# Fourteen weight pieces decoded in part two instead of part one, without the detour through DRAM

## The chip, the cores and the metric

The kernel runs on one core of a Trainium2 chip. The metric is device time in microseconds (us); lower is better. The kernel before takes 1982.79 us (median of 3 runs, 1981.26 to 1983.64). TensorE (PE) multiplies, VectorE (DVE) and ScalarE (ACT) do elementwise work, GpSimd (POOL) does next to nothing here, and SyncE's queue (SP) issues every DMA.

## What is computed

Three layers follow each other: a Fourier mix along the sequence (4 batches of 3072 tokens, 256 channels), an MoE-like layer with 2048 hidden units, and a channel mix with 1024 hidden units. Cut to what matters here:

```
X = rfft(x, axis=1);  Yr = Xr@w_r - Xi@w_i + b_r;  Yi = Xr@w_i + Xi@w_r + b_i
y = irfft(softshrink(Yr, 0.01) + 1j*softshrink(Yi, 0.01))     # 4 x 3072 x 256
h = y @ w_in;  g = h * tanh(softplus(h));  z = g @ w_out      # w_in 256x2048, w_out 2048x256
zk, zr = mixes of z with the token before it
out = sigmoid(zr @ w_g) * (relu(zk @ w_k)**2 @ w_v)            # w_k 256x1024, w_v 1024x256, w_g 256x256
```

The function h*tanh(softplus(h)) is one ScalarE function, Mish. The weights of the last two layers (w_in, w_out, w_k, w_v, w_g) come as 64-bit floats, which no engine multiplies. They are turned on the chip into two 32-bit tiles each, a rounded high part and the low rest, and every product is taken as three matmuls (high by high, high by low, low by high).

## The kernel before

**Part one** does the Fourier mix in 48 units (`u`), 12 for each batch: matmuls `xps`, `yps` and `bps` on PE, with ScalarE and VectorE between them. Its results go to DRAM (`b_dr`). A background queue of VectorE work (`bg`: `f1_ops` ahead of the transform, `f3_ops` behind it) fills VectorE between the units; `f3_ops` turns `b_dr` into `y_dr` in jobs of half a batch each, in a tile of the pool `g`.

**Part two** does the two other layers in 24 blocks (`j`) of 512 tokens. A block has 16 steps, and step `s` is block `s // 16`. At step `s` the program writes, engine by engine, what belongs to it:

- PE: `emit_H(s)`, six matmuls into a PSUM tile `hps`; then what the table `PLAN` puts at this step (`emit_K`: six matmuls into `kps`; `emit_V`: twelve into `v`; `emit_R`); then `emit_acc(s - 3)`, six matmuls into `a` from `gh`, `gl` and the tile of `w_out` for that step. `hps`, `kps` and `zps` share a ring of four PSUM tiles.
- ScalarE: `act_mish(s - 1)` reads `hps` and writes `u`, and behind it stand the operations that an earlier step left with `later`: `evac` of the block before (`x2s`), `token_mix` (`t`), `split_y` of the next block (`yh`), and the three of a `K` group (`ka`, `kh`, `ka`).
- VectorE: `dve_g(s - 1)` writes `gh` (a cast of `u`) and `gl` (`u` minus `gh`). One operation of the list `vx` is put behind `gh`, one behind `gl`, and the rest after that; where `vx` is empty, `bg` gives one.

In the first block only `H` and `acc` run; its first `K` group stands at step 22, and needs the mixed tokens `xk` from steps 19 and 20.

**Decoding.** Weights are decoded in pieces of 128x512 numbers; `w_in` and `w_out` have eight each, `w_k` and `w_v` four each, `w_g` one. `raw_piece` loads 512 KB into `raw`; `decode` gives six stages. On VectorE: `v0` (an integer operation and a shift-and-or that build `q`), `v1` (`q` limited, times the sign `sg`), `v2` (the low part; two halves for `w_out`). On ScalarE: `a0` (a copy of the high words into `sg`, then Sign), `a1` (Abs of `q`), `a2` (the high part; two halves for `w_out`). The class `Weights` runs pieces as a pipeline: each call of `vec` starts a piece's `v0`, does `v1` of the piece before, and `v2` of the third before; `sca` does `a2` of the second before, `a0` and `a1` of the new one, and loads the next raw piece.

In the kernel before, all 25 pieces are decoded in part one. Five (`w_k` and one of `w_v`) come at units 6 to 14, the other twenty at units 36 to 47, two per unit. The SBUF that `w_k`, `w_v` and `w_g` will use is still taken there, so these nine pieces are written to DRAM (`park_piece`, `w_dr`), and `fetch` reads them back at the start of part two, with 5 DMAs of 512 KB and 16 of 128 KB. In part two there is no decoding.

The helpers on lines 146 (`tt`), 149 (`stt`), 152 (`act`) and 155 (`mm`) issue most instructions, so the profile shows their lines for nearly everything, and groups are told apart by the names of their tiles. In the changed kernel the same helpers stand two lines further down.

Of the kernel before, what the change touches and what calls it, by code (L numbers as in the profile page):

```python
# [10 lines left out]
F32 = mybir.dt.float32  # L11
# [25 lines left out]
START = (20500, 20500)  # L37
SLACK = (2000, 3200)

NPARK = 5  # L40
PARK_AT = (6, 15)

F3_PART1 = {(1, 4): [(0, 0)], (1, 8): [(0, 1)]}
F3_PART2 = {1: (1, 0), 3: (1, 1), 5: (2, 0), 8: (2, 1), 10: (3, 0), 14: (3, 1)}


SPLIT_AT = (13, 14)
# [66 lines left out]
def tile_fft_mix_moe_channel_mix(  # L114
# [41 lines left out]

    dram = pool(ctx, "dram", 1, space=bass.MemoryType.DRAM)
    b_dr = [dram.tile([2, 128, NT, 256], F32, name=f"b_dr{b}") for b in range(NB)]
    w_dr = [dram.tile([128, 2, 512], F32, name=f"w_dr{i}") for i in range(9)]
    y_dr = [dram.tile([2, 128, 24, 128], F32, name=f"y_dr{b}") for b in range(NB)]  # L160

    cst = pool(ctx, "cst", 1)
# [272 lines left out]

    raws = []

    def raw_piece(src):
        p, tag = raws[1][raws[0] % len(raws[1])]
        raws[0] += 1  # L440
        raw = p.tile([128, 512, 2], I32, tag=tag, name="raw", bufs=2)
        nc.sync.dma_start(out=raw.rearrange("p (k f) t -> p k (f t)", k=2),
                          in_=src.bitcast(I32).rearrange("(k p) f -> p k f", p=128))
        return raw

    def decode(raw, parts, scale=1.0):
        hw, lw = raw[:, :, 1], raw[:, :, 0]
        tl = {}

        def a0():  # L450
            sg = tl["sg"] = pools["st"].tile([128, 512], F32, tag="sg", name="sg")
            return [lambda: act(sg.bitcast(I32), hw.bitcast(F32), ACTF.Copy, scale=14000.0),
                    lambda: act(sg, sg.bitcast(I32), ACTF.Sign)]

        def v0():
            q = tl["q"] = pools["st"].tile([128, 512], F32, tag="q", name="q", bufs=3)
            qi = q.bitcast(I32)
            return [lambda: V.tensor_scalar(out=qi, in0=hw, scalar1=0x08000000, scalar2=3,
                                            op0=ALU.bitwise_xor, op1=ALU.logical_shift_left),
                    lambda: stt(qi, lw, 29, qi, ALU.logical_shift_right, ALU.bitwise_or)]  # L460

        def a1():
            return [lambda: act(tl["q"], tl["q"], ACTF.Abs)]

        def v1():
            return [lambda: stt(tl["q"], tl["q"], 3.4e38, tl["sg"], ALU.min, MULT)]

        def a2():
            tl["p"] = parts(tl["q"])
            return [lambda hi=hi, v=v: act(hi, v, ACTF.Copy, scale=scale) for hi, lo, v in tl["p"]]  # L470

        def v2():
            if scale == 1.0:
                return [lambda hi=hi, lo=lo, v=v: tt(lo, v, hi.bitcast(F32), SUB) for hi, lo, v in tl["p"]]
            return [lambda hi=hi, lo=lo, v=v: stt(lo, v, scale, hi.bitcast(F32), MULT, SUB)
                    for hi, lo, v in tl["p"]]

        return a0, v0, v1, a2, v2, a1

    def win_piece(i):  # L480
        raw = raw_piece(w_in[:, 256 * i:256 * i + 256])
        cs = slice(256 * i, 256 * i + 256)
        w = wt["in"]
        return decode(raw, lambda q: [(w[:, 0, :, cs], w[:, 1, :, cs],
                                q.rearrange("p (k f) -> p k f", k=2))])

    def wout_piece(i):
        raw = raw_piece(w_out[256 * i:256 * i + 256, :])

        def parts(q):  # L490
# [3 lines left out]
        return decode(raw, parts)  # L494


    parked = ([w_k[:, 256 * i:256 * i + 256] for i in range(4)]
              + [w_v[256 * i:256 * i + 256, :] for i in range(4)] + [w_g])

    def park_piece(i):  # L500
        raw = raw_piece(parked[i])
        tl = {}

        def parts(q):
            t = tl["t"] = yhl_p.tile([128, 2, 512], F32R, tag="yl", name="wp")
            return [(t[:, 0, :], t[:, 1, :], q)]
        a0, v0, v1, a2, v2, a1 = decode(raw, parts)
        return a0, v0, v1, a2, lambda: v2() + [lambda: nc.sync.dma_start(out=w_dr[i], in_=tl["t"].bitcast(F32))], a1

    def fetch():  # L510
        for i in range(4):
            nc.sync.dma_start(out=wt["v"][:, :, 2 * i:2 * i + 2, :].bitcast(F32),
                              in_=w_dr[4 + i].rearrange("p s (c f) -> p s c f", c=2))
        nc.sync.dma_start(out=wt["g"].bitcast(F32), in_=w_dr[8].rearrange("p s (c f) -> p s c f", c=2))
        for c in range(8):
            wt["k", c] = mat.tile([128, 2, 2, 128], F32R, tag="m", name="wkt")
            src = w_dr[c // 2].rearrange("p s (h k f) -> p s h k f", h=2, k=2)
            for z in range(2):
                nc.sync.dma_start(out=wt["k", c][:, z].bitcast(F32), in_=src[:, z, :, c % 2, :])

    class Weights:

# [48 lines left out]
    def part1():  # L571
        with ExitStack() as es:
# [163 lines left out]
            for u in range(NU):  # L736
                b, t = divmod(u, NT)
                if t == NT - 1 and b + 2 < NB:
                    new_a(b + 2)
                if t == F1_AT[b] and b + 1 < NB:  # L740
                    hs = [f1_ops(As[b + 1], h) for h in range(2)]
                    for i, due in ((slice(14), 0), (slice(14, 24), 4), (slice(24, None), 8)):
                        bg.add(both(*[(h[0] + h[1])[i] for h in hs]), NT * (b + 1) + due)
                bg.jobs += F3_PART1.get((b, t), [])
                bg.step()
                if u == NU - NT - 1:
                    wt["in"] = big.tile([128, 2, 2, 2048], F32R, tag="big", name="win")
                    todo = [lambda: win_piece(0)]
                    for i in range(8):
                        if i < 7:  # L750
                            todo.append(lambda i=i: win_piece(i + 1))
                        todo.append(lambda i=i: wout_piece(i))
                    late = [lambda i=i: park_piece(i) for i in range(NPARK, 9)]
                    wq = Weights(todo[:6] + late + todo[6:])
                    wq.load(3)
                dec = 0
                if b == NB - 1:
                    dec = 2
                elif PARK_AT[0] <= u < PARK_AT[1]:
                    dec = 1  # L760
                    if u == PARK_AT[0]:
                        wq = Weights([lambda i=i: park_piece(i) for i in range(NPARK)])
                        wq.load(2)
                bg.flush(u + 1)
                if u == 6:
                    S.activation(out=mu1, in_=mu, func=ACTF.Copy, scale=-1.0, bias=1.0)
                pe += 1710 * (u + 1 < NU)
                if u + 1 < NU:
                    emit_F(u + 1)
                if u:  # L770
                    post_M(u - 1)
                if dec:
                    emit(wq.vec())
                    bg.clock += 2100
                if u:
# [11 lines left out]
                if dec == 2:  # L787
                    emit(wq.vec())
                    emit(wq.sca(2))
                    bg.clock += 2100  # L790
                emit_M(u)
                pe = max(pe, x_at + 300) + 2770
                y_new = pe + 700
                if u:
                    emit_I(u - 1)
                    pe = max(pe, y_at + 300) + 1710
                x_at, y_at = x_next, y_new
                if b == NB - 1 and t == 10:
                    bg.drain()
                    load_y(0)  # L800
            while wq.busy():
                emit(wq.vec())
                emit(wq.sca(2))
            for h in range(2):
                emit(split_y(0, h)[1])
            post_M(NU - 1)
            post_M2(NU - 1)
            post_I(NU - 2)
            emit_I(NU - 1)
            post_I(NU - 1)  # L810
# [2 lines left out]
    def part2():  # L813
        with ExitStack() as es:
# [18 lines left out]
            xr = (xr_p.tile([128, 2, 512], F32R, name="xrh"), xr_p.tile([128, 2, 512], F32R, name="xrl"))  # L833
            xs = x2_p.tile([128, 1088], F32, name="x2s")[:, 0:1026].rearrange("p (h f) -> p h f", h=2)

            fetch()
            NC = 16
            h_t, u_t, gh, acc, kt = {}, {}, {}, {}, {}
            vps, rt, mix_t = {}, {}, {}
# [137 lines left out]
            for s in range(max(max(plan), max(fin_at)) + 2):  # L977
                j, c = divmod(s, NC)
                if s < NS:
                    if c == 10 and j + 1 < NBLK:  # L980
                        load_y(j + 1)
                    if j in F3_PART2 and c == 0:
                        bg.jobs.append(F3_PART2[j])
                    bg.step()
                    emit_H(s)
                ax, vx = defer.pop(s, ([], []))
# [12 lines left out]
                    act_mish(s - 1)  # L999
                for e in ax:  # L1000
                    e()
                vx = list(vx)
                bg.have = min(bg.have + FILL[0], FILL[1])

# [62 lines left out]
```

## Time and profile before

| what | value |
|---|---|
| median of 3 runs | 1982.79 us |
| profiled execution, its own time | 1981.86 us |
| its span in the trace | 1979.9 us |
| PE busy | 1958.0 us, 99% of the span |
| DVE busy | 1141.4 us, 58% |
| ACT busy | 929.0 us, 47% |
| first matmul of part two | 327.22 us |

All times inside an execution count from the span's start. The time outside the span is 1.96 us. The granted TensorE clock is 1.00 in every slice of the page, so it plays no part. Where a row ends in brackets, they hold the idle time of that engine just before the row, and what ended it. A start-to-start distance of two rows is often a little shorter than the first row's duration, since an engine overlaps the end of one instruction with the start of the next.

### The profile page before, as it was taken

The numbers are of one execution on the slowest core, as the hardware profiler recorded it, in microseconds if no ns is written. First come the engines' busy times: TensorE is split into PE (matmuls) and PEld (weight loads), VectorE is DVE, ScalarE is ACT, GpSimd is POOL, SyncE is SP. The second block draws the span as 40 slices with busy tenths as digits, with TensorE's granted clock in tenths as the row PEclk, the third lists the DMA queues.
The fourth block names the chain that finished last, engine by engine and source line by source line (L and its number), as shares of the span: only waits on it lengthen the run. The fifth ranks groups of instructions, "written<-read, shape, count | busy, mean of one in ns | idle before, by whom it ended". The sixth has DMA issues, their size and how long they took to land.

```text
span 1979.9 us, 25685 instructions
## 1 busy us (share of the span) xinstructions
PE 1958.0 (99%) x10084; PEld 1686.2 (85%) x10084; DVE 1141.4 (58%) x2183; ACT 929.0 (47%) x1525; POOL 13.2 (1%) x28
## 2 busy tenths in 40 slices
PE   6999999999999999999999999999999999999999
PEld 5888888888888888888888888888888888888888
DVE  8999976665654754465375445555544544444444
ACT  2422286344544554454445444444544544454455
POOL 0000000000000000000000000000000000000000
PEclk9999999999999999999999999999999999999999
DMA  9445276111011010101101001011000000000000
GB/s 279 150 138 170 70 245 200 39 32 65 22 33 54 22 44 11 54 22 33 54 22 54 1 22 54 5 33 38 22 1 22 22 11 12 22 23 1 22 11 22
DMA packets 104554, 106.66 MB, mean 54 GB/s; under 512 B 7017, under 2 KB 85489, under 8 KB 103409
## 3 DMA queue, kind: packets, MB, share of 16 engines
q1 hardware_dynamic: 104432, 105.02, 16.7%
q8 instruction: 79, 1.29, 0.3%
q14 instruction: 43, 0.34, 0.1%
HBM read 62.53 MB, written 42.47 MB: 53 GB/s over the span
## 4 chain that ended last, share of the span: by engine, by line
PE 97%; DMA 1%; DVE 1%; ACT 0%; issue 0%; SPq 0%; DVEq 0%; ACTq 0%
PE a L155 26%; PE hps L155 26%; PE v L155 14%; PE kps L155 13%; PE yps L155 7%; PE bps L155 4%; PE xps L155 4%; PE zps L155 3%; DMA a<-in_x_dram 1%; DMA w_dr<-wp 0%; DVE g L146 0%; ACT sg L152 0%; SPq L266 0%; DVE q L149 0%; ACT q L152 0%
## 5 line engine op out<-in xcount | busy, mean ns | idle before, releaser
L863 DVE CAST gh<-u 128x512 fp32r<-128x512 f32 x384 | 163.2, 425 | 747.5 <-PE a L155 598.2
L155 PE MATMUL a<-gh,wo 128*128 128x512 f32 x1536 | 536.3, 390 | 0.0
L155 PE MATMUL hps<-yh,win 128*128 128x512 f32 x1536 | 534.7, 389 | 0.0
L152 ACT ACTIVATE u<-hps 128x512 f32<-128x512 f32 x384 | 229.7, 598 | 525.0 <-PE hps L155 368.8
L155 PEld LDWEIGHTS hps<-yh,win 128*128 128x128 f32 x1536 | 288.3, 188 | 60.3
L155 PEld LDWEIGHTS a<-gh,wo 128*128 128x128 f32 x1536 | 288.4, 188 | 58.0
L155 PE MATMUL a<-gl,wo 128*128 128x512 f32 x768 | 299.9, 390 | 0.0
L155 PE MATMUL hps<-yl,win 128*128 128x512 f32 x768 | 298.8, 389 | 0.0
L155 PE MATMUL kps<-b,wkt 128*128 128x512 f32 x960 | 280.1, 390 | 0.0
L155 PE MATMUL v<-b,kh 128*128 128x256 f32 x1536 | 275.8, 281 | 0.0
L146 DVE TENSOR_TENSOR gl<-u,gh 128x512 fp32r<-128x512 f32 x384 | 263.6, 687 | 3.6
L155 PEld LDWEIGHTS v<-b,kh 128*128 128x128 f32 x1536 | 243.7, 190 | 7.6
L155 PE MATMUL v<-b,kl 128*128 128x256 f32 x768 | 215.8, 281 | 0.0
L155 PEld LDWEIGHTS kps<-b,wkt 128*128 128x128 f32 x960 | 179.1, 188 | 36.1
L152 ACT ACTIVATE ka<-kps 128x512 f32<-128x512 f32 x192 | 115.0, 599 | 185.5 <-PE kps L155 185.5
L155 PEld LDWEIGHTS hps<-yl,win 128*128 128x128 f32 x768 | 144.1, 188 | 29.9
L155 PEld LDWEIGHTS a<-gl,wo 128*128 128x128 f32 x768 | 144.5, 188 | 26.6
L146 DVE TENSOR_TENSOR kl<-ka,kh 128x512 fp32r<-128x512 f32 x192 | 132.5, 690 | 32.8 <-ACT ka L152 19.1
L155 PEld LDWEIGHTS v<-b,kl 128*128 128x128 f32 x768 | 144.1, 188 | 0.0
L152 ACT ACTIVATE ka<-ka 128x512 f32<-128x512 f32 x192 | 121.4, 632 | 6.3
L152 ACT ACTIVATE kh<-ka 128x512 fp32r<-128x512 f32 x192 | 121.4, 632 | 6.3
L146 DVE TENSOR_TENSOR g<-g 128x128 f32<-128x128 f32 (+3 forms) x272 | 107.5, 433 | 1.2
(80 smaller groups left out, 1926.8 us busy)
## 6 DMA issues: line engine op xcount, KB each, us to landing
b_dr<-bs SPq DMA_DIRECT2D x48, 256.0 KB, 2.2
g<-b_dr SPq DMA_DIRECT2D x8, 1536.0 KB, 6.8
y<-y_dr SPq DMA_DIRECT2D x48, 256.0 KB, 3.2
out_dram<-r SPq DMA_DIRECT2D x48, 256.0 KB, 2.2
y_dr<-g SPq DMA_DIRECT2D x80, 64.0 KB, 1.6
w_dr<-wp SPq DMA_DIRECT2D x9, 512.0 KB, 5.9
a<-in_x_dram SPq DMA_DIRECT2D x8, 512.0 KB, 6.2
y_dr<-g SPq DMA_DIRECT2D x32, 128.0 KB, 1.9
```

What stands on the lines that cost most here:

```text
L146: V.tensor_tensor(out=o, in0=a, in1=b, op=op)
L152: S.activation(out=o, in_=i, func=f, **kw)
L155: T.matmul(out=o, lhsT=l, rhs=r, start=start, stop=stop, **kw)
L863: return [lambda: V.tensor_copy(hi, u), lambda: tt(lo, u, hi.bitcast(F32), SUB)]
```

## The change

- Eleven pieces (eight of `w_in`, three of `w_out`) stay in part one, one per unit from unit 34 on. The other fourteen (five of `w_out`, then four of `w_k`, four of `w_v`, one of `w_g`) are decoded in part two, one every second step from step 0 to step 26, and their pipeline ends at step 32.
- `park_piece`, `fetch` and the tiles `w_dr` go. The decoded parts are written where the matmuls read them.
- The decode's working tiles in part two are slices of one tile of the pool `g` (named `stage`): one slot for `sg`, three for `q`, two for `raw`. In part one `sg` keeps its two buffers.
- The `f3_ops` jobs of part two start at given steps instead of given blocks. The first moves from step 16 to step 34, the second from step 48 to 50; the others keep theirs.
- At the end of part one the last `yb` is written before the first block's `split_y`.

```diff
-NPARK = 5
-PARK_AT = (6, 15)
+NWO = 3
+DEC_STEPS = range(0, 34, 2)
-F3_PART2 = {1: (1, 0), 3: (1, 1), 5: (2, 0), 8: (2, 1), 10: (3, 0), 14: (3, 1)}
+F3_PART2 = {34: (1, 0), 50: (1, 1), 80: (2, 0), 128: (2, 1), 160: (3, 0), 224: (3, 1)}
...
+    def stage(tag, bufs):
+        if "slots" in pools:
+            slots, at = pools["slots"]
+            at[tag] += 1
+            return slots[tag][at[tag] % len(slots[tag])]
+        return pools["st"].tile([128, 512], F32, tag=tag, name=tag, bufs=bufs)
...
         def a0():
-            sg = tl["sg"] = pools["st"].tile([128, 512], F32, tag="sg", name="sg")
+            sg = tl["sg"] = stage("sg", 2)
             return [lambda: act(sg.bitcast(I32), hw.bitcast(F32), ACTF.Copy, scale=14000.0),
                     lambda: act(sg, sg.bitcast(I32), ACTF.Sign)]
...
-                    late = [lambda i=i: park_piece(i) for i in range(NPARK, 9)]
-                    wq = Weights(todo[:6] + late + todo[6:])
+                if u == NU - NT - 3:
+                    wq = Weights([lambda i=i: win_piece(i) for i in range(8)] +
+                                 [lambda i=i: wout_piece(i) for i in range(NWO)])
                     wq.load(3)
...
+            post_M(NU - 1)
+            post_M2(NU - 1)
             for h in range(2):
                 emit(split_y(0, h)[1])
-            post_M(NU - 1)
-            post_M2(NU - 1)
...
-            fetch()
+            for c in range(8):
+                wt["k", c] = mat.tile([128, 2, 2, 128], F32R, tag="m", name="wkt")
+            G = g_p.tile([128, 8, 512], F32, tag="g", name="stage")
+            slots = {"sg": [G[:, 0, :]], "q": [G[:, i, :] for i in (1, 2, 3)],
+                     "raw": [G[:, 4:6, :], G[:, 6:8, :]]}
+            pools["slots"] = (slots, dict.fromkeys(slots, 0))
+            wq = Weights([lambda i=i: wout_piece(i) for i in range(NWO, 8)] +
+                         [lambda i=i: wk_piece(i) for i in range(4)] +
+                         [lambda i=i: wv_piece(i) for i in range(4)] + [wg_piece])
+            wq.load(2)
...
+                if s in DEC_STEPS and wq.busy():
+                    vx = wq.vec() + list(vx)
+                    later(s + 1, wq.sca(2), [])
```

What this does to the order, at two places. First ScalarE where part two begins. `bs` are the last results of part one, `hps` what PE gives to Mish, `u` what Mish writes; before, these rows stand there:

```order
L152 ACTIVATE yb_2720<-yps_2695 128x512
L152 ACTIVATE bs_2723<-bps_2709 128x512
L152 ACTIVATE bs_2731<-bps_2726 128x512
L152 ACT_TABLE_LOAD
L152 ACTIVATE u_2825<-hps_2811 128x512
L152 ACTIVATE u_2838<-hps_2818 128x512
L152 ACTIVATE u_2851<-hps_2831 128x512
L152 ACTIVATE u_2872<-hps_2844 128x512
```

Now there is a decode between every second pair of Mish operations; this is the fourth piece (steps 7 to 9), where `stage` without `hps` is a stage of the decode, and `wo` a piece of `w_out`:

```order
L154 ACTIVATE u_2701<-hps_2669 128x512
L154 ACTIVATE u_2727<-hps_2694 128x512
L154 ACTIVATE wo_2703<-stage_2575 128x256
L154 ACTIVATE wo_2704<-stage_2575 128x256
L154 ACTIVATE stage_2575<-stage_2575 128x512
L154 ACT_TABLE_LOAD
L154 ACTIVATE stage_2575<-stage_2575 128x512 x2
L154 ACT_TABLE_LOAD
L154 ACTIVATE u_2752<-hps_2720 128x512
```

Sign and Abs (the `x2`) stand between two table loads: Mish and Sign are in different tables. The whole program has 77 table loads instead of 49.

The second place is VectorE at the same steps. Before, only `gh` and `gl` stand there:

```order
L863 CAST gh_2912<-u_2910 128x512
L146 TENSOR_TENSOR gl_2913<-u_2910,gh_2912 128x512
L863 CAST gh_2931<-u_2929 128x512
L146 TENSOR_TENSOR gl_2932<-u_2929,gh_2931 128x512
L863 CAST gh_2950<-u_2948 128x512
```

Now `v2` (`wo`), `v1` (the first row that only names `stage`) and `v0` (the two behind it) stand among them:

```order
L863 CAST gh_2756<-u_2752 128x512
L148 TENSOR_TENSOR wo_2703<-stage_2575,wo_2703 128x256
L148 TENSOR_TENSOR gl_2757<-u_2752,gh_2756 128x512
L148 TENSOR_TENSOR wo_2704<-stage_2575,wo_2704 128x256
L151 SCALAR_TENSOR_TENSOR stage_2575<-stage_2575 128x512
L469 TENSOR_SCALAR stage_2575<-stage_2575 128x512
L151 SCALAR_TENSOR_TENSOR stage_2575<-stage_2575 128x512
L863 CAST gh_2786<-u_2778 128x512
L148 TENSOR_TENSOR gl_2787<-u_2778,gh_2786 128x512
```

So `v1` of a piece now stands on VectorE behind the `gh` and `gl` that read a `u` which ScalarE writes after that piece's Abs. And since `sg` has one slot, the ScalarE copy that starts the next piece is made to wait in the built program for exactly this `v1`.

## Rows read from the trace of the kernel before

**Rows 1.** The page, section 1: engine, busy us (share of span), instructions.

```profile
PE 1958.0 (99%) x10084; PEld 1686.2 (85%) x10084; DVE 1141.4 (58%) x2183; ACT 929.0 (47%) x1525; POOL 13.2 (1%) x28
```

**Rows 2.** Timeline, PE: start us, us, engine, line, instruction, [idle before <-releaser].

```profile
293.47 1.99 PE L155 MATMUL bps<-im,yb 128*128 128x256 f32 x8 [0.26 <-DVE yb L149]
...
332.86 0.39 PE L155 MATMUL a<-gh,wo 128*128 128x512 f32 x1
...
384.54 1.52 PE L155 MATMUL kps<-b,wkt 128*128 128x512 f32 x6
...
395.42 1.52 PE L155 MATMUL kps<-b,wkt 128*128 128x512 f32 x6
```

**Rows 3.** Timelines of SP (two issues) and VectorE (first use); landing of `raw`.

```profile
246.01 1.01 SPq L442 DMA_DIRECT2D raw<-in_moe_w_in_dram  x2
...
328.73 2.57 SPq L512 DMA_DIRECT2D b<-w_dr  x4
...
250.13 0.43 DVE L458 TENSOR_SCALAR q<-raw 128x512 int32<-128x512 int32 x1 [3.60 <-DMA raw<-in_moe_w_in_dram]
...
DMA to landing us min/median/max: 3.8/5.4/7.1
```

**Rows 4.** Timeline, ScalarE: one piece's decode in part one.

```profile
310.59 0.71 ACT L152 ACTIVATE wo<-q 128x256 fp32r<-128x256 f32 x2
311.20 0.66 ACT L152 ACTIVATE sg<-raw 128x512 int32<-128x512 f32 x1
311.89 0.63 ACT L152 ACTIVATE sg<-sg 128x512 f32<-128x512 int32 x1
312.43 0.62 ACT L152 ACTIVATE q<-q 128x512 f32<-128x512 f32 x1
```

**Rows 5.** Timeline, ScalarE: the table load where part two begins.

```profile
327.65 0.60 ACT L152 ACTIVATE bs<-bps 128x512 f32<-128x512 f32 x1 [1.18 <-PE bps L155]
328.27 1.28 ACT L152 ACT_TABLE_LOAD   x1
329.56 0.60 ACT L152 ACTIVATE u<-hps 128x512 f32<-128x512 f32 x1
```

**Rows 6.** Timeline, VectorE: the decode's operations, `gh`, `gl`, and a half-width operation.

```profile
309.42 0.69 DVE L149 SCALAR_TENSOR_TENSOR q<-q,sg 128x512 f32<-128x512 f32 x1 [0.26 <-ACT q L152]
310.03 0.42 DVE L458 TENSOR_SCALAR q<-raw 128x512 int32<-128x512 int32 x1
310.48 0.69 DVE L149 SCALAR_TENSOR_TENSOR q<-raw,q 128x512 int32<-128x512 int32 x1
...
330.20 0.43 DVE L863 CAST gh<-u 128x512 fp32r<-128x512 f32 x1 [4.72 <-ACT u L152]
...
420.43 0.43 DVE L863 CAST gh<-u 128x512 fp32r<-128x512 f32 x1 [2.27 <-PE a L155]
420.78 0.42 DVE L146 TENSOR_TENSOR g<-g 128x256 f32<-128x256 f32 x1
421.11 0.69 DVE L146 TENSOR_TENSOR gl<-u,gh 128x512 fp32r<-128x512 f32 x1
```

**Rows 7.** Timeline, VectorE and then ScalarE: a token mix, and a `u` that waited.

```profile
380.84 0.74 DVE L149 SCALAR_TENSOR_TENSOR t<-x2s,mu,t 128x512 f32<-128x512 f32 x1
381.50 0.68 DVE L146 TENSOR_TENSOR gl<-u,gh 128x512 fp32r<-128x512 f32 x1
382.10 0.42 DVE L895 CAST b<-t 128x512 fp32r<-128x512 f32 x1
382.56 0.69 DVE L146 TENSOR_TENSOR b<-t,b 128x512 fp32r<-128x512 f32 x1
...
382.30 0.60 ACT L152 ACTIVATE u<-hps 128x512 f32<-128x512 f32 x1 [2.35 <-DVE gl L146]
```

**Rows 8.** Timeline, ScalarE: the first and last operation of a `K` group.

```profile
386.54 0.59 ACT L152 ACTIVATE ka<-kps 128x512 f32<-128x512 f32 x1
...
387.82 0.64 ACT L152 ACTIVATE ka<-ka 128x512 f32<-128x512 f32 x1
```

More of the change, by code (lines that the diff above doesn't have):

```diff
@@ L158, in tile_fft_mix_moe_channel_mix @@
     b_dr = [dram.tile([2, 128, NT, 256], F32, name=f"b_dr{b}") for b in range(NB)]
-    w_dr = [dram.tile([128, 2, 512], F32, name=f"w_dr{i}") for i in range(9)]
     y_dr = [dram.tile([2, 128, 24, 128], F32, name=f"y_dr{b}") for b in range(NB)]
@@ L436, in tile_fft_mix_moe_channel_mix @@
     raws = []
-    def raw_piece(src):
-        p, tag = raws[1][raws[0] % len(raws[1])]
-        raws[0] += 1
-        raw = p.tile([128, 512, 2], I32, tag=tag, name="raw", bufs=2)
+    def stage(tag, bufs):
[4 more added lines that the diff above has]
+        return pools["st"].tile([128, 512], F32, tag=tag, name=tag, bufs=bufs)
+    def raw_piece(src):
+        if "slots" in pools:
+            raw = stage("raw", 2).bitcast(I32).rearrange("p a f -> p (a f)").rearrange("p (f t) -> p f t", t=2)
+        else:
+            p, tag = raws[1][raws[0] % len(raws[1])]
+            raws[0] += 1
+            raw = p.tile([128, 512, 2], I32, tag=tag, name="raw", bufs=2)
         nc.sync.dma_start(out=raw.rearrange("p (k f) t -> p k (f t)", k=2),
@@ L455, in v0 @@
         def v0():
-            q = tl["q"] = pools["st"].tile([128, 512], F32, tag="q", name="q", bufs=3)
+            q = tl["q"] = stage("q", 3)
             qi = q.bitcast(I32)
@@ L482, in win_piece @@
         cs = slice(256 * i, 256 * i + 256)
-        w = wt["in"]
-        return decode(raw, lambda q: [(w[:, 0, :, cs], w[:, 1, :, cs],
+        return decode(raw, lambda q: [(wt["in"][:, 0, :, cs], wt["in"][:, 1, :, cs],
                                 q.rearrange("p (k f) -> p k f", k=2))])
@@ L494, in wout_piece, with wk_piece, wv_piece, wg_piece @@
         return decode(raw, parts)
[L497 to L502, printed above, removed]
-        def parts(q):
[L505 to L519, printed above, removed]
+    def wk_piece(i):
+        raw = raw_piece(w_k[:, 256 * i:256 * i + 256])
+        def parts(q):
+            z = q.rearrange("p (k f) -> p k f", k=2)
+            return [(wt["k", 2 * i + c][:, 0, :, :], wt["k", 2 * i + c][:, 1, :, :],
+                     z[:, :, 128 * c:128 * c + 128]) for c in range(2)]
+        return decode(raw, parts)
+    def wv_piece(i):
+        raw = raw_piece(w_v[256 * i:256 * i + 256, :])
+        w = wt["v"][:, :, 2 * i:2 * i + 2, :]
+        return decode(raw, lambda q: [(w[:, 0], w[:, 1], q.rearrange("p (c f) -> p c f", c=2))])
+    def wg_piece():
+        raw = raw_piece(w_g)
+        w = wt["g"]
+        return decode(raw, lambda q: [(w[:, 0], w[:, 1], q.rearrange("p (c f) -> p c f", c=2))])
     class Weights:
@@ L747, in part1 @@
                     wt["in"] = big.tile([128, 2, 2, 2048], F32R, tag="big", name="win")
[L748 to L752, printed above, removed]
-                    late = [lambda i=i: park_piece(i) for i in range(NPARK, 9)]
-                    wq = Weights(todo[:6] + late + todo[6:])
-                    wq.load(3)
[L756 to L763, printed above, removed]
+                if u == NU - NT - 3:
+                    wq = Weights([lambda i=i: win_piece(i) for i in range(8)] +
+                                 [lambda i=i: wout_piece(i) for i in range(NWO)])
+                    wq.load(3)
+                dec = u > NU - NT - 3
                 bg.flush(u + 1)
@@ L786, in part1 @@
                     post_I(u - 2)
[L787 to L790, printed above, removed]
                 emit_M(u)
@@ L981, in part2 @@
                         load_y(j + 1)
-                    if j in F3_PART2 and c == 0:
-                        bg.jobs.append(F3_PART2[j])
+                    if s in F3_PART2:
+                        bg.jobs.append(F3_PART2[s])
                     bg.step()
```

## The prediction

> **What bounds the kernel now.** I read the page first: PE is busy for 1958.0 of 1979.9 us, VectorE for 58% and ScalarE for 47% [rows 1]. Then I went through PE's timeline where pieces are decoded today, units 36 to 47 of part one. PE sat idle there once, for 0.26 us, waiting for VectorE [rows 2]. So today's decode hides behind PE, and so does the detour through DRAM: no row of PE waits for it. Any time that PE loses in part two is added to the end, because behind the first two blocks PE is full again and catches up nothing. The question is therefore only whether the other engines can do the decode inside the first 28 steps as fast as PE goes through them.
>
> PE's pace comes from two rows. Between the first `K` group and the third stand eight groups of six matmuls, and they take 395.42 - 384.54 = 10.88 us [rows 2]: 1.36 a group. A step without K or V is two groups, 2.72 us, so a pair of steps, in which one piece is decoded, lasts 5.44 us.
>
> **What is removed.** The idle 0.26 us may go: -0.3. The fourteen pieces' work in part one, nine DMAs to DRAM and 21 back were hidden; they give nothing. The new order at the end of part one is `yb` first and `split_y` after, and those four operations last about as long as the last `bps` group; I take 0, at most 0.5. The later `f3_ops` job falls into steps where VectorE's average load is 58% [rows 1]; 0 to 1.
>
> **The start of part two.** `v0` of the first piece is the first thing on VectorE, ahead of `gh` of step 0, and it waits for its raw data. SP is in order, and these loads stand behind the last `b_dr` store, where the first `fetch` DMA was issued at 328.73. In part one a raw issue at 246.01 was first used at 250.13, 4.1 us later [rows 3]. So the data are there at T = 332.9; with the longest landing, 7.1 us [rows 3], at 335.8. Before, the first `acc` began at 332.86 [rows 2], so some stall is certain at once.
>
> **The cost of one piece on ScalarE.** From the copy into `sg`: 0.69 to Sign's place [rows 4], a table load of 1.29 start to start [rows 5], 0.54 from Sign to Abs, 0.62 for Abs with 0.02 before the next load (as behind `bs`) [rows 4, 5], again 1.29, then Mish. That makes D = 0.69 + 1.29 + 0.54 + 0.64 + 1.29 = 4.45 us. With two Mish operations about 0.5 apart (Sign to Abs is 0.54) and the two halves of `w_out` (0.61) [rows 4] ScalarE has 1.0 + 0.61 + 4.45 = 6.06 us of work a pair, more than PE's 5.44 already.
>
> The Trainium skill speaks against this change here: "ScalarE: Activation LUTs", section "Table sets: the hidden batching unit", says to group activations by table set and to do all of one set before switching. The 1.28 us of the load agree with its section "What ACT_TABLE_LOAD costs" (1283 ns); it adds a drain of some 1380 ns to every switch, but here the load starts 0.02 us after the end of `bs`, and Mish 0.01 us after the load [rows 5]. By its figure D would be some 2.7 us longer, an estimate; I go by the rows.
>
> **The loop that makes it worse.** `sg` has one slot. The copy of a new piece must wait for `v1` of the piece before, and `v1` stands on VectorE behind `gh` and `gl` of a `u` that ScalarE writes only after that piece's second table load. So decode and Mish cannot overlap. From the start of that `u`: 0.64 to `gh` (329.56 to 330.20) [rows 5, 6]; 0.35 to the first `v2` half, 0.33 to `gl` (as with the half-width operation at 420.78) [rows 6]; 0.60 to the second half (as behind `gl` at 381.50) [rows 7]; 0.33 to `v1`; 0.69 for `v1`; 0.12 until ScalarE goes on (`gl` ends at 382.18, `u` starts at 382.30) [rows 7]. Sum 3.06, and then D: **7.51 us a pair, against PE's 5.44**. For the second and third piece there is no `v2` yet, and `gh` to `v1` is 0.35: 0.64 + 0.35 + 0.69 + 0.12 + 4.45 = 6.25.
>
> **The sum along this chain**, counted from T, with `u` numbered by its step:
> - u1 at 4.45; u3 and u5 after two short loops: 16.95.
> - Six loops to u17: 45.06, and a `split_y` copy inside one of them (0.5): 62.5.
> - To u19 a token mix stands ahead of the table load (0.6): 70.6.
> - The mix runs on VectorE late. Its `t` starts on ScalarE at loop time 6.2 and ends at 6.8; then t, `gl`, cast, subtract at 0.66, 0.60, 0.46 and 0.6 [rows 7] end at 9.2, and only then comes the next `gh`: 1.08 behind u19 instead of 0.64. From there 0.35 + 0.33 + 0.60 + 0.33 to `v1`, 0.61 to its neighbour, 0.45 + 0.61 for `v0` [rows 6], then the second half of the mix, 0.66 + 0.46 + 0.69: at 6.2 behind u19 `xk` is complete.
> - The first `K` group can start at T + 70.6 + 6.2 = T + 76.8 = 409.7, where it stood at 384.54: **25.2 us late**.
> - u21 comes 0.44 late: +7.95, 78.6. Before u23 the three operations of a `K` group stand ahead of the table load (386.54 to 388.46, 1.92) [rows 8]: +9.3, 87.9. The third `K` group writes the PSUM tile that u23 frees: T + 87.9 + 0.65 = 421.4 against 395.42: 26.0 late. The group in step 29 waits in the same way for u27, by my count 0.3 us more.
>
> After step 29 no table loads are left but those of Sigmoid, and PE is full again. So the profiled execution of 1981.86 becomes 1981.86 - 0.3 + 26.3 = 2007.9; its time lies 0.93 below the median, which is within the spread of the runs. I predict **2008 us** (+1.3%). Own range: T can be 2.9 later and 0.3 earlier; the nine loops each 0.3 off either way, 2.7; the small terms of the second paragraph +1.5. That is 2004 to 2014.
>
> **Rivals.**
> - *ScalarE's sum alone decides*: if `v1` is never waited for (VectorE ahead of ScalarE, or the wait satisfied early), the loop is 6.06. Then u17 comes at 53.3, u19 (with the `evac` pair, no longer in a gap) at 61.0, `K` at T + 67.2 = 400.1, 15.6 late: 1997 us. The wait is in the built program, and `v1` cannot pass `gh` on its engine; against it. 7%.
> - *The switch is hidden, not slower than before*: if a table load ran while ScalarE waits for VectorE and PE, D would shrink to 0.69 + 0.54 + 0.54 = 1.8 and the loop to about 4.8 us. The point that decides is 5.44: below it PE sets the pace. Only the start is left: `gh` at T + 1.06 and `gl` 0.46 + 0.69 later stand where PE wanted them, at 332.86 and one matmul (0.23) later: some 2 us. Time 1981.86 - 0.3 + 2 = 1983.6, which is no difference that can be measured. Against it: the load in [rows 5] fills ScalarE's time between two operations fully. 3%.
> - *A switch costs twice as much*: a drain as long as the load, 1.28 more a switch, 2.56 a piece. Ten pieces stand before u19, so `K` is 25.6 later than above, and the next two pieces carry 5 more to u23, of which PE's own work hides nothing: 2008 + 31 = 2039. This is what the drain in the Trainium skill, "ScalarE: Activation LUTs", section "What ACT_TABLE_LOAD costs", would do. [Rows 5] show none. 3%.
> - *The change doesn't do what it says*: excluded, as the order shows the loads, and 77 table loads.
>
> **How the numbers follow.** The forecast has 86%, the rivals 7, 3 and 3%, and 1% is for a time that is shorter than before for a reason I don't see. Of the forecast's 86% I put 80 between 2001 and 2014, a little below its own lower end, since small overlaps on ScalarE (0.1 us in each of 30 switches) can add up; to reach further, to 1997 or to 2039, would take in more than 8 times in 10. About 0.2% (4 us) is what a measurement of this kernel can tell from no change: faster by more than that 1%, within it 3%, slower 96%.
>
> **What would show each step.** First use of the raw data near 333. ScalarE nearly full between 335 and 425, with two table loads every 7.5 us, and a wait for VectorE ahead of the copy into `sg`. First `kps` near 410, third near 421. PE's idle time between 330 and 430 about 26 us in sum, first on `gh` and `gl`, later on `xk` and on Mish's PSUM tile; none behind step 30, and part two beginning at 327 as before. The prediction is wrong if the copy into `sg` starts at once after Mish (6.1 us loops), if Mish or Sign start more than 0.1 us behind a load, or if PE stalls after step 30.

## The result, and the profile after

The changed kernel takes **2007.31 us** (median of 4 runs, 2006.83 to 2007.61) where the kernel before takes 1982.30 us in the same comparison (4 runs, 1981.26 to 1983.64). The ratio is 1.0126, with a 95% interval of 1.011 to 1.0142: it is slower by 25 us. The prediction was 2008 us, with a range of 2001 to 2014.

| what | before | after |
|---|---|---|
| profiled execution, its own time | 1981.86 us | 2007.39 us |
| span | 1979.9 us | 2005.4 us |
| PE busy | 1958.0 us, 99% | 1968.3 us, 98% |
| ScalarE busy | 929.0 us, 47% | 965.4 us, 48% |
| first matmul of part two | 327.22 us | 326.60 us |
| third `K` group | 395.42 us | 420.39 us |

The page's row of busy times, and under it the groups of table loads on ScalarE (count, busy us, mean ns), after. [Rows 1] have the row of before.

```profile
PE 1968.3 (98%) x10084; PEld 1688.5 (84%) x10084; DVE 1140.1 (57%) x2187; ACT 965.4 (48%) x1557; POOL 13.6 (1%) x28
...
L154 ACT ACT_TABLE_LOAD x77 | 98.8, 1283 | 10.6 <-DMA braw<-in_b_r_dram 9.3
```

ScalarE's share of the whole span hardly moved, from 47 to 48%. The loss is visible only in the stretch where the work went. These are the busy times of the engines in stretches of 30 us, after (stretch, its length, then PE, PEld, VectorE, ScalarE and POOL, granted TensorE clock, DMA share, GB/s):

```profile
330.00:360.00 30.00, 26.54 (x102) 19.60 (x101) 16.73 (x34) 24.24 (x35) 0.00 (x0) 0.94 0.32 103
360.00:390.00 30.00, 24.00 (x90) 17.31 (x89) 18.25 (x38) 25.01 (x39) 0.00 (x0) 0.94 0.27 88
390.00:420.00 30.00, 24.49 (x98) 18.92 (x96) 18.98 (x38) 26.76 (x39) 0.00 (x0) 0.94 0.23 71
420.00:450.00 30.00, 29.60 (x152) 25.13 (x153) 21.57 (x40) 25.95 (x42) 0.71 (x1) 1.00 0.06 18
```

For 90 us ScalarE is busy for 81 to 89% while PE waits for 3.5 to 6 us of every 30; from 420 on PE is full again. What PE waited for between 326 and 470 us stands in its waits (engine, tile, line, releaser: us in total, times, longest):

```profile
PE a L157 <- DVE gl L148: 5.2, 7, 3.0
PE a L157 <- DVE gh L863: 3.4, 4, 1.4
PE a L157 <- ACT x2s L154: 2.5, 1, 2.5
PE kps L157 <- DVE b L895: 1.9, 1, 1.9
PE kps L157 <- ACT u L154: 1.3, 1, 1.3
PE hps L157 <- DVE yl L148: 0.7, 1, 0.7
PE kps L157 <- DVE b L148: 0.2, 1, 0.2
```

The same view of the kernel before is empty. The names are VectorE's in all but two rows, yet VectorE is busy for only some 17 to 19 us of each 30: it hands on a lateness that comes from ScalarE. How, is to be read in one loop of the decode. ScalarE's timeline after, from the copy into `sg` of one piece to the copy of the next (start, length, instruction, [idle before <-releaser]):

```profile
352.05 0.67 ACT L154 ACTIVATE stage<-stage 128x512 int32<-128x512 f32 x1 [1.32 <-issue]
352.73 1.28 ACT L154 ACT_TABLE_LOAD   x1
354.03 1.15 ACT L154 ACTIVATE stage<-stage 128x512 f32<-128x512 int32 x2
355.20 1.28 ACT L154 ACT_TABLE_LOAD   x1
356.49 1.09 ACT L154 ACTIVATE u<-hps 128x512 f32<-128x512 f32 x2
357.47 0.72 ACT L154 ACTIVATE wo<-stage 128x256 fp32r<-128x256 f32 x2
359.51 0.68 ACT L154 ACTIVATE stage<-stage 128x512 int32<-128x512 f32 x1 [1.32 <-issue]
```

And VectorE's in the same loop:

```profile
357.12 0.43 DVE L863 CAST gh<-u 128x512 fp32r<-128x512 f32 x1 [3.03 <-ACT u L154]
357.47 0.42 DVE L148 TENSOR_TENSOR wo<-stage,wo 128x256 fp32r<-128x256 f32 x1
357.80 0.69 DVE L148 TENSOR_TENSOR gl<-u,gh 128x512 fp32r<-128x512 f32 x1
358.40 0.42 DVE L148 TENSOR_TENSOR wo<-stage,wo 128x256 fp32r<-128x256 f32 x1
358.74 0.69 DVE L151 SCALAR_TENSOR_TENSOR stage<-stage 128x512 f32<-128x512 f32 x1
```

The two engines wait for each other in turn. VectorE idles 3.03 us until Mish has written `u`; then come `gh`, half of `v2`, `gl`, the other half, and `v1` (the last row), which ends at 359.43. ScalarE has nothing to do for 1.32 us and copies into `sg` at 359.51, 0.08 after `v1`. The profile puts that wait down to "issue", that is, to nothing it can name; seven such waits, of 1.20 to 1.41 us, add up to 9.2 us. From one copy to the next it is 359.51 - 352.05 = 7.46 us, against the 5.44 us that PE needs for a pair of steps.

### The profile page after: what moved, and what is told of

Its sections match the earlier page's. It is cut to its first block, busy times and chain, and to the rows that moved or that the text cites. A ratio compares the mean times of both kernels' runs of the same rounds, so it can differ in the third digit from the quotient of the medians.

```text
span 2005.4 us, 25689 instructions
## 1 busy us (share of the span) xinstructions
PE 1968.3 (98%) x10084; PEld 1688.5 (84%) x10084; DVE 1140.1 (57%) x2187; ACT 965.4 (48%) x1557; POOL 13.6 (1%) x28
## 4 chain that ended last, share of the span: by engine, by line
PE 79%; ACT 0%; DVE 0%; issue 0%; DVEq 0%; ACTq 0%
PE a L157 25%; PE hps L157 24%; PE v L157 13%; PE kps L157 13%; PE zps L157 3%; ACT L154 0%; ACT stage L154 0%; DVE t L151 0%; DVE xkl L148 0%; DVE r L148 0%; ACT x2s L154 0%; ACT ka L154 0%; ACT u L154 0%; DVE b L895 0%; ACT kh L154 0%
```

## The experiments

The theory has two parts: the two table loads of each piece fill ScalarE to 6.06 us a pair, and the single slot of `sg` makes it 7.5, because decode and Mish cannot overlap. The rivals to it: that the amount of decoding is too much for this place, whatever its tables are; that the stretch where the raw data are late costs what it costs; or that the small parts of the change (jobs moved, order at the seam) have a share. This table shows what was measured; the last column is the time from part two's first `hps` to its third `K` group in the profiled execution, and how much later that is than before. It leaves out that part two begins up to 1.5 us earlier or later from run to run.

| kernel | median us (range, runs) | ratio to before, 95% | third `K` group |
|---|---|---|---|
| before | 1982.30 (1981.26 to 1983.64, 4) | | 68.20 |
| after | 2007.31 (2006.83 to 2007.61, 4) | 1.011 to 1.0142 | 93.79, +25.6 |
| second slot for `sg` | 1997.43 (1997.34 to 1999.84, 4) | 1.0059 to 1.0093 | 84.51, +16.3 |
| `v1` ahead of `gh` | 1997.41 (1995.79 to 1998.11, 4) | 1.006 to 1.009 | 84.30, +16.1 |
| copies for Sign and Abs | 1985.58 (1984.91 to 1988.27, 10) | 1.0009 to 1.0028 | 72.06, +3.9 |
| raw data one unit earlier | 2004.67 (2004.00 to 2005.19, 4) | 1.0097 to 1.0128 | 91.06, +22.9 |
| signs on VectorE | 1986.98 (1984.93 to 1987.98, 11) | 1.0012 to 1.003 | 72.80, +4.6 |
| tables for five pieces only | 1995.94 (1995.20 to 1996.06, 4) | 1.0051 to 1.0082 | 82.48, +14.3 |
| two small parts alone | 1982.12 (1981.38 to 1984.74, 11) | 0.9991 to 1.0008 | 68.20, 0 |
| signs on VectorE, raw data earlier | 1981.88 (1981.62 to 1982.32, 11) | 0.9988 to 1.0006 | 68.60, +0.4 |

The first four experiments were compared with 13 runs of before (median 1982.3), the last four with 27 (median 1982.44).

### A second slot for `sg`

```diff
-            slots = {"sg": [G[:, 0, :]], "q": [G[:, i, :] for i in (1, 2, 3)],
+            R2 = sg_p.tile([128, 4, 256], F32, tag="r", name="stage2").rearrange("p a f -> p (a f)")
+            slots = {"sg": [G[:, 0, :], R2[:, 0:512]], "q": [G[:, i, :] for i in (1, 2, 3)],
```

> The changed kernel with a second slot for sg (in the tile that the sigmoid results use later), so that the copy of a new piece need not wait for v1 of the piece before. Theory (two table loads a piece in series with Mish, and the single sg slot that stops them from overlapping): the loop falls from 7.5 us a pair of steps to ScalarE's own sum, 6.06 us; the first K group comes near 399.5 instead of 408, and the time is about 1996.5 (1995 to 1998), 11 us less than the changed kernel's 2007.3. If the order on VectorE or the raw loads held the loop, and not the slot, it stays at 2006 to 2008.

ScalarE's timeline of this kernel, one loop:

```profile
350.26 1.09 ACT L154 ACTIVATE u<-hps 128x512 f32<-128x512 f32 x2
351.23 0.72 ACT L154 ACTIVATE wo<-stage 128x256 fp32r<-128x256 f32 x2
351.84 0.67 ACT L154 ACTIVATE stage<-stage 128x512 int32<-128x512 f32 x1
352.53 1.28 ACT L154 ACT_TABLE_LOAD   x1
353.82 1.16 ACT L154 ACTIVATE stage<-stage 128x512 f32<-128x512 int32 x2
355.00 1.28 ACT L154 ACT_TABLE_LOAD   x1
356.29 1.09 ACT L154 ACTIVATE u<-hps 128x512 f32<-128x512 f32 x2
```

No row has a wait, and the loop is 356.29 - 350.26 = 6.03 us. The time falls by 9.9 us, to 1997.43. So the wait for the slot was 10 of the 25 us, and what is left is mainly ScalarE's own sum, which the prediction had put at 6.06 us a pair and 1997 us. Not all of it: in the profile, counted from part two's start, PE is 14.7 us late behind the first `K` group, and 1.6 of the 16.3 us come on just behind that, with slow matmuls (below, under what was not expected).

### `v1` ahead of `gh`

One slot as in the change, but `v1` of the piece before is written on VectorE ahead of `gh`, so that ScalarE's copy finds `sg` free.

```diff
                 if s in DEC_STEPS and wq.busy():
-                    vx = wq.vec() + list(vx)
+                    old = wq.pipe[0]
+                    n = len(wq.pipe[2][4]()) if wq.pipe[2] else 0
+                    ops = wq.vec()
+                    if old:
+                        ops.pop(n)()
+                    vx = ops + list(vx)
```

> The changed kernel with one sg slot as it is, but v1 of the piece before written ahead of gh on VectorE instead of behind gl. Theory: v1 runs while VectorE would wait for Mish, so the slot is free when ScalarE comes to the next copy; the loop is 6.06 us as with two slots, and the time about 1996.5 (1995 to 1998). If the slot's wait is not what lengthens the loop, 2006 to 2008.

1997.41 us, the same as with a second slot. Here no memory is added and no work removed; one instruction stands elsewhere in VectorE's order. That the wait labelled "issue" goes with it shows that it was the wait for `v1`.

### Copies in place of Sign and Abs

```diff
-                    lambda: act(sg, sg.bitcast(I32), ACTF.Sign)]
+                    (lambda: act(sg, sg.bitcast(I32), ACTF.Copy, scale=2.0 ** -31)) if "slots" in pools else
+                    (lambda: act(sg, sg.bitcast(I32), ACTF.Sign))]
...
-            return [lambda: act(tl["q"], tl["q"], ACTF.Abs)]
+            f = ACTF.Copy if "slots" in pools else ACTF.Abs
+            return [lambda: act(tl["q"], tl["q"], f)]
```

> The changed kernel with Sign and Abs of the decode in part two replaced by two copies (scale 2^-31, and 1), which need no table load: the same number of instructions without the 28 added loads; it leaves out the sign, so the weights have the right size and a wrong sign. Theory: the loop is 3.06 + 0.69 + 0.54 + 0.54 = 4.8 us, below PE's 5.44, so PE sets the pace; what is left is the wait for the first raw piece (some 1.5 us) and up to 1.5 us where the token mix meets the decode on VectorE: 1982.5 to 1985. If the decode's work on VectorE and ScalarE itself were too much for these steps, 1990 or more.

As many instructions of the same size are left on ScalarE, and 49 table loads instead of 77. The time is 1985.58 us: 21.7 of the 25 us are gone. The decode's work is not too much for this place; its table loads are. Of the 21.7 us, 9.9 are the wait for the slot, by the two experiments above, and 11.8 go with the loads alone. The slot is still waited for in this kernel, but without the loads that does not delay PE. One pair of steps on ScalarE in this kernel, and PE's waits:

```profile
351.62 0.58 ACT L154 ACTIVATE u<-hps 128x512 f32<-128x512 f32 x1
354.12 0.60 ACT L154 ACTIVATE u<-hps 128x512 f32<-128x512 f32 x1 [1.92 <-PE hps L157]
...
356.98 0.58 ACT L154 ACTIVATE u<-hps 128x512 f32<-128x512 f32 x1
```

```profile
PE a L157 <- DVE gh L865: 1.3, 1, 1.3
PE kps L157 <- DVE b L897: 0.9, 1, 0.9
PE a L157 <- DVE gl L148: 0.3, 1, 0.3
PE kps L157 <- DVE b L148: 0.2, 1, 0.2
```

Now ScalarE waits for PE (1.92 us for `hps`), and 356.98 - 351.62 = 5.36 us is PE's pace. PE waits at two places only: 1.6 us where the raw data are late, 1.1 us for the token mix `b`, whose operations on VectorE stand among those of the decode. The time was 0.6 above the upper end of what was expected, 1985.

### The raw data one unit earlier

The working tile is made and the first two raw pieces are loaded in unit 46 of part one, right after `load_y(0)`, instead of at the start of part two.

```diff
                 if b == NB - 1 and t == 10:
                     bg.drain()
                     load_y(0)
+                    G = g_p.tile([128, 8, 512], F32, tag="g", name="stage")
...
+                    pools["wq"].load(2)
...
-            wq.load(2)
+            wq = pools["wq"]
```

> The changed kernel with the stage tile made, and the first two raw pieces loaded, one unit earlier, behind the load of y, so that they are there when part two begins. Theory: the whole chain begins at the end of the first Mish (329.5) instead of at the landing (332.2), and every loop follows: 2.7 us less, about 2004.6 (2004 to 2005.3). If the start is covered by later waits, no change: 2007.3.

2004.67 us, 2.64 less than the changed kernel. The raw data's lateness is a term of the sum in full, as long as ScalarE is the bound behind it: the first loop starts that much sooner, and all others with it.

### Signs on VectorE

The decode of part two takes the sign by an and-mask, and `v1` becomes an and and an or of integers. Sign, Abs and the copy into `sg` leave ScalarE.

```diff
+                more = [lambda: V.tensor_scalar(out=sg.bitcast(I32), in0=hw, scalar1=-0x80000000, scalar2=0,
+                                                op0=ALU.bitwise_and, op1=ALU.bitwise_or)]
...
+            if "slots" in pools:
+                return []
...
+                return [lambda: stt(qi, qi, 0x7fffffff, si, ALU.bitwise_and, ALU.bitwise_or)]
```

> The change, with the decode of part two taking its signs on VectorE (an and-mask into sg, then v1 as an and and an or of integers) and nothing of a0 and a1 left on ScalarE, so that 49 table loads are left, as before. If the table loads and the wait of the copy into sg behind v1 make the change slow, the place of the decode does not matter: 1983 to 1986 us, like the run with copies in place of Sign and Abs (1985.6), with PE waiting some 1.6 us where part two begins and some 1 us ahead of the first K group. If instead VectorE, which gets about 0.3 us more a pair of steps, now cannot keep up with PE's 5.44 us a pair: 1990 or more.

1986.98 us, 1.0 above the expected range. So the change's place for the decode costs 4.5 us, not 25, once its ScalarE operations need no other table. PE's listed waits are only at the start, 2.1 us. But the third `K` group is 4.6 us late, so the waits don't add up to the loss. PE's timeline shows the rest:

```profile
335.54 0.51 PE L157 MATMUL a<-gh,wo 128*128 128x512 f32 x1 [1.83 <-DVE gh L873]
...
338.21 0.63 PE L157 MATMUL a<-gh,wo 128*128 128x512 f32 x1
338.64 0.63 PE L157 MATMUL hps<-yh,win 128*128 128x512 f32 x1
```

Behind this wait and one of 0.29 us the matmuls start 0.43 us apart (338.21, 338.64) instead of 0.23, until 339.5. In the stretch from 336 to 340 us the granted clock is 0.57. This is told below, under what was not expected. Matched matmul by matmul with the trace of before, 2.7 of the 4.6 us come on at the two stops, 1.5 with the slow matmuls and 0.4 at the mix, where the drawn idle time (0.09 us) is too short to be listed.

### Tables for five pieces only

Sign and Abs are kept for the five pieces of `w_out` and replaced by copies for the other nine.

```diff
-        return decode(raw, parts)
+        return decode(raw, parts, free=True)
```

(for the pieces of `w_k`, `w_v` and `w_g`, where `free` takes the copies in place of Sign and Abs)

> The change with Sign and Abs kept for the five pieces of w_out alone; the nine other pieces of part two have copies in their place, so their signs are left out (59 table loads). If each loop of 7.5 us costs PE its 2 us when it runs, PE is late by what it is late in the changed kernel after the fifth piece, 366.02 against 357.56, that is 8.5 us, and nothing comes after but up to 1 us at the token mix: 1990.3 to 1992 us. If the loss is made mainly where the token mix and the K groups meet the table loads, behind step 19, it is like the run without any: 1985 to 1987.

1995.94 us: neither. The first half of the expectation holds: the `acc` of the fifth piece starts 366.46 - 326.79 = 39.67 us behind the first `hps`, where before it was 357.56 - 327.22 = 30.34, so 9.3 us are lost by then, the late raw data included (366.02 - 326.60 - 30.34 = 9.1 in the changed kernel). But 5 more are lost behind it, where I had expected at most 1: matched with the trace of before, 0.5 at the rest of the fifth loop, 1.0 and 1.8 at two waits at `split_y`, and 1.7 at the token mix, as much as the kernel with copies throughout loses there. The longest wait, in PE's timeline of this kernel:

```profile
379.82 0.50 PE L157 MATMUL hps<-yl,win 128*128 128x512 f32 x1 [1.52 <-DVE yl L148]
```

It is for `yl`, `split_y`'s low part for the next block, and stands behind the last table load. The kernel with copies throughout has neither wait at `split_y`. I take it that there the other engines had work done ahead, and that here five slow loops had used that lead up, so that whatever VectorE does besides `gh` and `gl` shows at once on PE; no run tests this by itself. The dose is clear in any case: 10 of the 28 loads bring back 10.4 of the 21.7 us.

### Two small parts alone

The kernel before, with the moved `f3_ops` jobs and with `yb` ahead of `split_y`:

```diff
-F3_PART2 = {1: (1, 0), 3: (1, 1), 5: (2, 0), 8: (2, 1), 10: (3, 0), 14: (3, 1)}
+F3_PART2 = {34: (1, 0), 50: (1, 1), 80: (2, 0), 128: (2, 1), 160: (3, 0), 224: (3, 1)}
...
-            for h in range(2):
-                emit(split_y(0, h)[1])
             post_M(NU - 1)
             post_M2(NU - 1)
+            for h in range(2):
+                emit(split_y(0, h)[1])
```

> The kernel before with two small parts of the change alone: the f3 jobs of part two started at the steps 34, 50, 80 and so on, and the last yb written ahead of split_y at the end of part one. The prediction put these at nothing: 1982.3 us, within 0.7. If the later first job or the order at the seam costs something, up to 1.5 us more: 1983.8.

1982.12 against 1982.44 us, ratio 0.9999 (0.9991 to 1.0008). They cost nothing that can be measured, as the prediction had it.

### Signs on VectorE, and the raw data earlier

Both edits of the two experiments above together.

> The run with signs on VectorE, and the first two raw pieces of part two loaded one unit earlier. If the 1.6 us that PE waits where part two begins come from the raw data alone, they go: 1.0 to 1.7 us less than the run with signs on VectorE, 1982.3 to 1984 us, level with the kernel before; not under it by over 0.5, since PE was full there. If VectorE's work ahead of gh at step 0 makes the wait and not the data, the two runs are the same within 0.5 us.

1981.88 against 1982.44 us, ratio 0.9997 (0.9988 to 1.0006): level with the kernel before. The gain over signs on VectorE alone is 5.1 us, more than the 1.0 to 1.7 expected: the stops at the start cost 2.7 us in the other kernel's profile, and the slow matmuls behind them, 1.5 us, go with them. PE's waits from 326 to 520 us are empty, as before; the 0.4 us that are left come on at the mix, where the drawn idle time is again 0.09 us. The stretch of the decode in this kernel, in the columns of the table by stretches:

```profile
330.00:360.00 30.00, 30.00 (x134) 24.87 (x133) 27.06 (x57) 10.90 (x24) 0.00 (x0) 1.00 0.40 123
360.00:390.00 30.00, 29.91 (x132) 24.44 (x132) 27.95 (x59) 13.67 (x28) 0.00 (x0) 1.00 0.29 88
```

PE is full, VectorE at 27 to 28 of 30 us, ScalarE at 11 to 14. So fourteen pieces can be decoded here at no cost. Nor is there anything to win: PE was full there before too. The one thing gained is traffic, by the page's line of the kernel before and then of this one:

```profile
DMA packets 104554, 106.66 MB, mean 54 GB/s; under 512 B 7017, under 2 KB 85489, under 8 KB 103409
```

```profile
DMA packets 97673, 97.22 MB, mean 49 GB/s; under 512 B 6536, under 2 KB 80912, under 8 KB 96528
```

9.4 MB less, which PE had not waited for (ScalarE had, twice, 7.4 us in all, for the stores to `w_dr`). No version was faster than the kernel before.

## Why the prediction was right, point by point

**The pace of PE, and what was hidden.** Right. The new order at the seam and the later jobs measured as nothing (0.9999). The DRAM detour's end gave no time, as the last experiment shows. PE's idle 0.26 us in part one is gone, but in the profiles of these kernels part two begins anywhere between 326.08 and 328.72 us, so the 0.3 us forecast for it can't be told from chance.

**The start.** The raw data were used first at 332.25 (5.28 us of VectorE waiting for them), 332.9 predicted. Part two itself began 0.6 earlier than before, so the distance was 5.65 where I had 5.68:

```profile
332.25 0.43 DVE L469 TENSOR_SCALAR stage<-stage 128x512 int32<-128x512 int32 x1 [5.28 <-DMA stage<-in_moe_w_out_dram]
```

**D and the loops.** Counted from the first copy into `sg` at 332.19, the start of `u` for some steps:

| step | predicted | measured |
|---|---|---|
| u1 | 4.45 | 4.46 |
| u5, after two short loops | 16.95 | 16.85 |
| u17, after six long ones | 62.5 | 62.2 |
| u19, with the mix ahead | 70.6 | 70.3 |
| u21 | 78.6 | 78.3 |
| u23, with a `K` group ahead | 87.9 | 87.6 |

The long loop is 7.45 to 7.48 us against 7.51, the short one 6.19 and 6.20 against 6.25. The sum held because each of its terms was a start-to-start distance from a row, and because the wait of the copy into `sg` behind `v1` was in it; without that wait it would have been the 1997 us of the first two experiments. Two of its figures don't follow from its own terms: u21 to u23 would be 7.51 + 1.92 = 9.43 where it has 9.3 (measured: 9.29), and the ends of the own range would be 2004.9 and 2015.0, not 2004 and 2014. Neither changes the outcome.

**The first `K` group.** The step that was wrong in its form. I let the group start when all of `xk` was there, at 409.7. It starts at 405.44 on the first half of `xk` and then waits for the second (start, length, matmuls, [idle before <-releaser]), after:

```profile
405.44 0.84 PE L157 MATMUL kps<-b,wkt 128*128 128x512 f32 x3
408.16 0.50 PE L157 MATMUL kps<-b,wkt 128*128 128x512 f32 x1 [1.88 <-DVE b L895]
408.88 0.73 PE L157 MATMUL kps<-b,wkt 128*128 128x512 f32 x2 [0.23 <-DVE b L148]
...
420.39 1.65 PE L157 MATMUL kps<-b,wkt 128*128 128x512 f32 x6 [1.26 <-ACT u L154]
...
446.95 1.52 PE L157 MATMUL kps<-b,wkt 128*128 128x512 f32 x6
```

Its last matmuls start at 408.88, when `xk` is complete, at 408.83 by VectorE's timeline and 408.7 by my count from u19. The slip did no harm because the end doesn't hang on this group: the third waits once more for `u` (1.26), the PSUM tile of u23, as predicted. It is 24.97 us later than in [rows 2], 25.6 counted from part two's start; 26.0 predicted. Then 0.46 comes on until the sixth group (446.95, where the trace of before has 421.52: 25.43). Of this 0.3 is the wait for u27, 0.3 predicted: the fifth group starts at 437.16, 0.05 behind the end of that `u` (436.51 + 0.60). Its drawn idle time is 0.01 us, so between 425 and 520 us PE's waits are empty, and behind it nothing more comes on.

**What I said would show it, and did not.** PE's idle time was to be 26 us in sum; its waits add up to 15.2, in 16 stops. The delay is 25.5 all the same. Two things fill the difference, neither in the prediction. First, a stop costs more than the idle time in brackets: matmuls at pace start 0.23 apart but are drawn 0.39 to 0.40 long, so a stop is counted only from the drawn end. In the kernel with copies, the fourth matmul of the first `K` group starts 388.27 - 386.56 = 1.71 behind the first instead of 0.69, which is 1.02 late, and 0.87 stands in its brackets; the fifth is 0.49 late with 0.23 in brackets, and the sixth 0.11 more (the last two are drawn 0.74 long together, where two at pace take 0.62):

```profile
386.56 0.84 PE L157 MATMUL kps<-b,wkt 128*128 128x512 f32 x3
388.27 0.49 PE L157 MATMUL kps<-b,wkt 128*128 128x512 f32 x1 [0.87 <-DVE b L897]
388.99 0.74 PE L157 MATMUL kps<-b,wkt 128*128 128x512 f32 x2 [0.23 <-DVE b L148]
```

Second, the granted clock fell three times (below), and matmuls that start 0.43 apart instead of 0.23 lose 0.20 us each. How much each of the two makes can be counted, since from the first `hps` on both traces have the same 8640 matmuls in the same order. Matched one by one, those of the changed kernel fall 26.04 us behind (part two began 0.62 earlier, which leaves 25.4). Of these, 19.9 come on at the sixteen stops, 0.3 a stop more than stands in the brackets; 1.2 at four stops whose drawn idle time is 0.05 us or less, which the waits don't list; and 4.9 where the clock was low. It is the same delay, seen from PE: ScalarE sets its length, and slow matmuls take the place of idle time. I had taken the clock to play no part because it played none before.

**The rivals.** *ScalarE's sum alone* was not this kernel, and its price came out as the first two experiments make it, 1997.4 us. That is partly luck: it had the first `K` group 15.6 us late, which is 14.7 in both profiles, and slow matmuls that it did not have add 1.6 and 1.4. *The switch is hidden*: no, the loads fill ScalarE's time, but taking them away gave 1985.6 where this rival had 1983.6; it had the start at 2 us, which cost 2.2, and had missed the wait for the mix, 1.7 us late with 1.1 in brackets. *A switch costs twice as much*: no. Behind each load the next operation starts 0.01 us after its end (356.49 behind 355.20 + 1.28), and a load starts 0.02 us behind the operation before it. The drain of some 1380 ns that the Trainium skill adds ("ScalarE: Activation LUTs", section "What ACT_TABLE_LOAD costs") is not seen: ahead of the 29 loads between 326 and 440 us ScalarE stood idle for 0.5 us in all, ahead of the 29 `u` for 0.2. The rule of the Trainium skill on the same page, section "Table sets: the hidden batching unit", to do all work of one table set before switching, is what this change broke. The copies in place of Sign and Abs show the price here, the slot's wait included: 21.7 us for 28 loads of 1.28, 36 us in sum. The rest lay in time in which ScalarE would have waited for PE (1.92 us in the pair shown of that kernel).

## What to carry to other kernels

Work that is moved beside other work brings its table with it: count the loads at the new place, and put the whole loop (both engines, with the slot that a piece holds until the other engine is through with it) against the pace of the engine that is full there, not the engine's average share. A wait for a slot can be as dear as the loads, and one instruction's place in the other engine's order removes it. A wait that a profile calls "issue" is settled by moving the suspected releaser, and the time that PE loses by stops is read from the distance of the same matmul in two traces, not from the sum of its idle times.

## What the runs showed of the hardware that was not expected

**The granted TensorE clock fell after short stops.** In the kernel before it is 1.00 in every stretch. After the change it is below 1 in three places, 334 to 342, 378 to 386 and 394 to 402 us; these are two stretches of 4 us there, in the columns given above (PE's busy time is the first number behind the comma, the clock the one ahead of the DMA share):

```profile
334.00:338.00 4.00, 3.71 (x10) 2.73 (x10) 1.26 (x3) 3.69 (x6) 0.00 (x0) 0.65 0.53 131
...
378.00:382.00 4.00, 2.50 (x6) 2.02 (x7) 3.23 (x7) 3.62 (x7) 0.00 (x0) 0.70 0.11 42
```

Ahead of each PE had stood still: for 1.40 and 0.29 us at 333 to 335, for 2.99 up to 379.5, for 2.55 up to 395.5. While it is low, matmuls start 0.43 us apart, the pace of the lower level (1.2 GHz), instead of 0.23, that of the higher (2.4 GHz). The stop alone does not decide it: the stop of 1.88 us at 408.16 was followed by no fall, nor were those of 1.33 and 0.30 in the profiled run of the kernel with copies, nor one of 2.25 at 379.56 in the kernel with a second slot.

**In these runs it costs time only where PE is the bound.** With a second slot for `sg` the clock was 0.61 from 338 to 342 us, with `v1` ahead of `gh` 1.00 throughout the same part, and yet PE is equally late behind the first `K` group, 14.7 us in both: ScalarE set the pace, and the slow matmuls lay in PE's waiting time. Behind that group PE waits no more in either kernel. There the clock fell in both, to 0.57 (402 to 406 and 398 to 402 us), and the 1.6 and 1.4 us that came on stayed to the end. In the two kernels where PE sets the pace throughout it is the same. Of the ten executions with copies, six have a mean clock of 1.000 and take 1984.91 to 1985.64 us, four have 0.999 and take 1986.52 to 1988.27. With signs on VectorE the three at 1.000 take 1984.93 to 1986.14, the eight at 0.999 1986.16 to 1987.98. So the kernel with signs on VectorE loses some 2.5 us with the clock up (1984.95, the middle of the three, against 1982.44) and some 4.7 with the clock down (1987.2, the middle of the eight), and nothing that can be measured once the raw data come earlier. The length of the stop itself was seen only in the profiled run, so a part of that difference may be longer stops. What decides whether the clock falls, these runs do not tell.
